# 400 slots in place of 448 for the first wide expert of a token-routed block, and the test that allows it

## The chip, the core and the metric

The kernel runs on one core of a Trainium2 chip. The metric is the device time of one execution in microseconds (us). Three runs of the kernel before gave 542.45, 544.16 and 544.39 us (median 544.16). The profile is of one more execution, which took 543.53 us by the same clock. Its span, from the first to the last instruction, is 541.8 us; the other 1.7 us lie around it.

## The reference

Three layers follow each other. What matters here is the second, a mixture of experts in which every token goes to exactly one of eight experts:

```python
# attention: 2 sequences x 12 heads x 448 tokens x 64  ->  x of 896 tokens x 768
logits = xn @ en.T / tau
expert_idx = np.argmax(logits, axis=1)
for e in range(E):                       # E = 8
    mask = expert_idx == e
    h = np.maximum(x[mask] @ w1[e], 0.0)       # 768 -> 1024
    out[mask] = gate_w[mask, None] * (h @ w2[e])   # 1024 -> 768
# third layer, all 896 tokens: h = x @ w_in (768 -> 2048), g = s * relu(h)**2 + b, g @ w_out (2048 -> 768)
```

Everything is float32. How many tokens an expert gets depends on the inputs. Evaluated on its default inputs (seed 0), the reference sends 3, 7, 31, 25, 387, 3, 9 and 431 tokens to experts 0 to 7; in the first sequence alone, expert 4 has the most (382 of 448).

## The kernel before

**Attention** fills the first 118 us or so: per pair of heads, scores, tanh, exponentials, sums and the product with v, with the routing logits collected on the way.

**Routing** (lines 490 to 601) counts the tokens of each expert (`cnt`), gives every token a slot number, and sorts the 896 tokens by expert: first the expert with the most tokens in the first sequence (rank 0, called R0), then the small ones, last the largest of the others (rank 1, R1). VectorE (DVE) writes the slot list `idx`, by which GpSimd (POOL) gathers the token rows out of DRAM in seven indirect transfers (line 559). It also writes a small table `tab` with the expert, the first slot, the count and a start for copying back for each rank, and a flag `rare`. Every engine reads `rare` later (line 833) and takes one of two courses: `rest(True)`, the common one, when exactly six experts have 32 tokens or fewer and none has over 448; otherwise `rest(False)`, which finishes any distribution. Both are the same function with another argument, written out twice.

**The experts.** The gathered rows are transposed into `xs` (tokens as columns, 768 features as six tiles of 128). All products are made of three float32r matmuls on a high and a low half (`mm3`, lines 638 to 641), so that a 128x128 weight tile against 448 tokens is three matmuls with 448 columns. R0 always takes slots 0 to 447 and R1 slots 448 to 895, in eight hidden tiles of 128 each: `layer1` (line 701) is 18 matmuls from `xs` into one PSUM bank `hw`, then a relu on ScalarE (ACT, line 717) and the low half on DVE (line 718); `layer2` (line 720) is 18 matmuls from those halves into six PSUM banks `y0` to `y5`. Slots that belong to another expert are overwritten afterwards. Stage `s` of the loop in `rest` (line 840) makes `layer1` of tile `s` and `layer2` of the tile before; stage 0 (`layer1` of R0's tile 0, line 824) is made before the courses part. Stages 1 to 7 are R0, 8 to 15 R1. In stage 8 `layer2` of R0's last tile and its copy out of PSUM (`put_wide`, line 726, by the helper `put`, lines 685 and 687) follow.

**The small experts** have a stretch of 32 slots each. Their two layers (`narrow1`, line 779; `narrow2`, line 795) are put into given stages by the table `STAGE`, as plain float32 matmuls with 32 stationary columns.

**Weights** come in 768 KB transfers from SyncE's (SP) queue into twelve slots in two rings (`rawa`, and the front of `mem`); `pump` issues the next one of a fixed list as soon as a slot's former tile has been used. ACT and DVE split each tile into its halves (`split`, lines 621 to 623).

**The boundary** (lines 870 to 926): the small expert of rank 2 ends, some of R1's neighbours' results are kept aside, and the third layer's input is split into halves (`split_y`), in the common course for the first 448 slots before R1's last `layer2`, so that ACT and DVE work beneath it. The third layer follows to the end.

Of the kernel before, what the change touches and what calls it, by code (L numbers as in the profile page):

```python
# [14 lines left out]
ALU = mybir.AluOpType  # L15
AX = mybir.AxisListType
# [5 lines left out]
B, H, S, D = 2, 12, 448, 64  # L22
NT = B * S
DM = H * D
E = 8
F1 = 1024
F2 = 2048
NF1 = F1 // 128
# [18 lines left out]

NARROW = 32
BACK = 224


GATES = "ppppaaa"
# [7 lines left out]
def tile_kernel(ctx, tc, qk, vp, emb, scal, wp, wi, wo, out, dbg=None):  # L60
    nc = tc.nc
    pe, dve, act, pool, sp = nc.tensor, nc.vector, nc.scalar, nc.gpsimd, nc.sync
# [17 lines left out]
    cnt = const.tile([TQ, E], F32, name="cnt")  # L80
# [7 lines left out]
    rr = const.tile([1, 4], F32, name="rr")  # L88
    isn, back = tv[:, 0], tv[:, 1]
    tab = const.tile([1, 4, E], I32, name="tab")  # L90
    rare = const.tile([1, 1], I32, name="rare")
# [407 lines left out]
    def warm(n):  # L499

        t = ps_x.tile([128, 2, 512], F32, tag="xt", name="warm")
        for _ in range(n):
            pe.matmul(out=t[:, 0, 0:128], lhsT=ident, rhs=ident)
# [42 lines left out]
        pe.matmul(out=iv, lhsT=cm[:, i], rhs=ao[:, 0, i], start=(i == 0), stop=False)  # L546
        pe.matmul(out=iv, lhsT=cm[:, i], rhs=ao[:, 1, i], start=False, stop=(i == NI - 1))
    warm(6)
    dve.tensor_scalar(out=isn, in0=cnt[0:1], scalar1=float(NARROW), scalar2=None, op0=ALU.is_le)
    dve.tensor_copy(out=idx, in_=iv)  # L550

    dve.tensor_reduce(out=rr[:, 0:1], in_=isn, axis=AX.X, op=ALU.add)
    dve.tensor_reduce(out=rr[:, 1:2], in_=cnt[0:1], axis=AX.X, op=ALU.max)
    dve.tensor_scalar(out=rr[:, 2:3], in0=rr[:, 0:1], scalar1=float(E - 2), scalar2=None, op0=ALU.not_equal)
    dve.tensor_scalar(out=rr[:, 3:4], in0=rr[:, 1:2], scalar1=float(S), scalar2=None, op0=ALU.is_gt)
    dve.tensor_tensor(out=rare, in0=rr[:, 2:3], in1=rr[:, 3:4], op=ALU.max)

    xg_t = [mem_y[:, j * DM:(j + 1) * DM] for j in range(NS)]
    rows_in += [pool.indirect_dma_start(out=xg, out_offset=None, in_=xd[:, :],
# [34 lines left out]
    for p in range(2):  # L594
        dve.tensor_scalar(out=idx2[:, p], in0=iv, scalar1=2.0, scalar2=float(p), op0=ALU.mult, op1=ALU.add)
    dve.tensor_scalar(out=back, in0=off[0:1], scalar1=-float(BACK), scalar2=0.0, op0=ALU.add, op1=ALU.max)
    for k, row in ((1, off[0:1]), (2, cnt[0:1]), (3, back)):
        dve.tensor_tensor(out=rv[:, k], in0=rm, in1=bc(row, E, 1), op=ALU.mult)
    with nc.allow_low_precision(reason="whole numbers below 1000"):
        dve.tensor_reduce(out=tab, in_=rv, axis=AX.X, op=ALU.add)  # L600
    xctx.close()


# [17 lines left out]
    def split(src, w, lo=dve):  # L621
        act.copy(out=w[0], in_=src)
        lo.tensor_tensor(out=w[1], in0=src, in1=w[0], op=ALU.subtract)

    def split1(u, f, lo=dve):
        key = (u, 0, f // 2)
        src = raw_t[key].rearrange("p (q k c j) -> p c k q j", q=4, k=KD, c=2)[:, f % 2]
        split(src, [t.rearrange("p k (q j) -> p k q j", q=4) for t in W1[f % 2]], lo)
        if f % 2:
            done(key)  # L630

    def split2(u, f, lo=dve):
        key = (u, 1, f // 2)
        split(raw_t[key].rearrange("p (c k f) -> p c k f", c=2, k=KD)[:, f % 2], W2[f % 2], lo)
        if f % 2:
            done(key)

    def mm3(out, ah, al, bh, bl, start, stop, **kw):
        pe.matmul(out=out, lhsT=ah, rhs=bh, start=start, stop=False, **kw)  # L639
        pe.matmul(out=out, lhsT=ah, rhs=bl, start=False, stop=False, **kw)  # L640
        pe.matmul(out=out, lhsT=al, rhs=bh, start=False, stop=stop, **kw)  # L641
# [41 lines left out]
    def put(i, out, in_):  # L683
        if i == 0:
            act.copy(out=out, in_=in_)
        else:
            dve.tensor_copy(out=out, in_=in_)


    def accs():  # L690
        return [ps_y.tile([128, 512], F32, tag=f"y{k}", name=f"y{k}") for k in range(KD)]

    def at(o, n):
        return slice(o, o + n) if isinstance(o, int) else bass.ds(o, n)

    def within(o, low):
        if isinstance(o, int):
            return o
        return nc.s_assert_within(o, 0, NT - low - 1, skip_runtime_bounds_check_because="the expert has more tokens here")

    def layer1(f, n, low, o, hw=hw):


        o = within(o, low)
        wh, wl = W1[f % 2]
        if f == 0 and hw is hn:

            for k in range(KD):
                for w in (wh, wl):
                    pe.matmul(out=hw[:, 0:n], lhsT=w[:, k], rhs=xs[0][:, k, at(o, n)], start=(k == 0 and w is wh), stop=False)  # L710
            for k in range(KD):
                pe.matmul(out=hw[:, 0:n], lhsT=wh[:, k], rhs=xs[1][:, k, at(o, n)], start=False, stop=(k == KD - 1))
        else:
            for k in range(KD):
                mm3(hw[:, 0:n], wh[:, k], wl[:, k], xs[0][:, k, at(o, n)], xs[1][:, k, at(o, n)], k == 0, k == KD - 1)
        hh, hl = (t[:, 0:n] for t in H2[f % 2])
        act.activation(out=hh, in_=hw[:, 0:n], func=ACTF.Relu)
        dve.scalar_tensor_tensor(out=hl, in0=hw[:, 0:n], scalar=0.0, in1=hh, op0=ALU.max, op1=ALU.subtract)

    def layer2(f, n, acc):  # L720
        wh, wl = W2[f % 2]
        hh, hl = (t[:, 0:n] for t in H2[f % 2])
        for k in range(KD):
            mm3(acc[k][:, 0:n], wh[:, k], wl[:, k], hh, hl, f == 0, f == NF1 - 1)

    def put_wide(n, low, o, acc, cnt=None):

        o = within(o, low)
        for k in range(KD):
            yk = y[k % 2][:, k // 2]  # L730
            if cnt is not None:
                keep = scr[:, k % 2 * 224:(k % 2 + 1) * 224]
                rest = yk[:, bass.ds(nc.s_assert_within(o + cnt, 0, NT, skip_runtime_bounds_check_because="slots of an expert"), 224)]
                put(k % 2, keep, rest)
            put(k % 2, yk[:, at(o, n)], acc[k][:, 0:n])
            if cnt is not None:
                put(k % 2, rest, keep)

    def put_last(acc, kept, o_back):
# [3 lines left out]
        for i in range(2):  # L743
            put(i, y[i][:, :, bass.ds(o_back, BACK)], kept[i])

# [23 lines left out]
    def tokens32(r):  # L769
        o = tabv(1, r, NT, [ENG.DVE])  # L770
        dve.tensor_tensor(out=x32, in0=xs[0][:, :, bass.ds(o, 32)], in1=xs[1][:, :, bass.ds(o, 32)], op=ALU.add)
# [31 lines left out]
    def convert(nm, f, out):  # L803

        t = raw_t[nm, f]
        lo, hi = t[:, :, 0], t[:, :, 1]
        o = out.bitcast(I32)
        dve.tensor_scalar(out=o, in0=hi, scalar1=3, scalar2=0x3FFFFFF8, op0=ALU.logical_shift_left, op1=ALU.bitwise_and)
        dve.scalar_tensor_tensor(out=o, in0=hi, scalar=-0x40000000, in1=o, op0=ALU.bitwise_and, op1=ALU.bitwise_or)  # L809
        dve.scalar_tensor_tensor(out=o, in0=lo, scalar=29, in1=o, op0=ALU.logical_shift_right, op1=ALU.bitwise_or)  # L810
        done((nm, f))
# [4 lines left out]
    def cube(t):  # L816
        return t.rearrange("p (k f) -> p k f", k=KD)
# [18 lines left out]

    def rest(fast):

        acc = accs()
        for s in range(1, 2 * NF1):  # L840
            f = s % NF1
            kind, r = STAGE.get(s - 1, (0, 0))
            if kind == 1:
                tokens32(r)
            if s == 2 * NF1 - 2:
                convert("wi", 0, wc0)
                split(cube(wc0), nw)
            elif s == 2 * NF1 - 1:
                convert("wi", 1, wc)
            u, o_ = ("R1", NT - S) if s >= NF1 else ("R0", 0)  # L850
            if s + 1 < 2 * NF1:
                split1("R1" if s + 1 >= NF1 else "R0", (s + 1) % NF1)
            split2(u, f)
            pump()
            if kind:
                (narrow1 if kind == 1 else narrow2)(r)
                pump()

            layer1(f, S, 0, o_)
            if f:  # L860
                layer2(f - 1, S, acc)
            if s == NF1:
                layer2(NF1 - 1, S, acc)
                put_wide(S, 0, 0, acc)
                acc = accs()
            if s >= NF1 and tys:
                r = max(tys)
                put_narrow(tys[r], tabv(1, r, NT, [ENG.Activation, ENG.DVE]))
                last_ty.append(tys.pop(r))
# [19 lines left out]

        o_back = tabv(3, 1, NT - BACK, [ENG.Activation, ENG.DVE])  # L890
        kept = raw_tile(("kept", 0), "b")[:, 0:6 * BACK].rearrange("p (i k t) -> p i k t", i=2, k=3)
        kept = [kept[:, i] for i in range(2)]
        for i in range(2):
            put(i, kept[i], y[i][:, :, bass.ds(o_back, BACK)])

# [7 lines left out]
        else:  # L903
# [3 lines left out]
            for r in range(E):  # L907
                n = tabv(2, r, NT, allc)
# [108 lines left out]
        for n in range(2 * NF):  # L1017
            p, f = divmod(n, NF)
# [25 lines left out]
    with tc.If(rare_v < 1):  # L1044
        rest(True)
# [59 lines left out]
```

## Time and profile before

| | |
|---|---|
| runs | 542.45, 544.16, 544.39 us |
| profiled execution | 543.53 us, span 541.8 us |
| mean granted TensorE clock | 0.987 of full speed |
| TensorE (PE) matmuls | 515.1 us busy, 95% of the span |
| PE weight loads | 418.1 us, 77% |
| DVE, ACT, POOL | 61%, 43%, 8% |
| DMA | 93.42 MB, 172 GB/s on average |

Busy shares are averages over stages with different limits. A row of the trace in order of time gives the start and the length of an instruction, or of several merged ones with their count; a bracket at its end gives how long the engine had been idle before it and what ended that. The ends of matmuls are modelled and neighbours overlap, so the pace of a row of matmuls is read from their starts. L with a number is a line of the kernel before.

### The profile page before, as it was taken

The page shows a single profiled execution, that of the slowest core. Times are in us where ns is not written, and L with a number is a line of the kernel's source. Part 1 is how long each engine was busy: PE and PEld are TensorE (multiplying, and loading weights), DVE is VectorE, ACT ScalarE, POOL GpSimd, SP SyncE. Part 2 cuts the span into 40 slices and gives each one's busy share as a digit, 9 for nine tenths or more (in the row PEclk, how much of TensorE's full clock was granted, in tenths as well). Part 3 has the DMA queues.
Part 4 walks back from the last instruction along what each step waited for, and adds up shares of the span by engine and source line. Part 5 has one row for each costly group of instructions (what it writes and reads, how often), then busy time and mean ns, then how long its engine had stood idle before and what let it go on. Part 6 is the DMA issues. An engine that isn't in the chain of part 4 may idle for free.

```text
span 541.8 us, 7919 instructions
## 1 busy us (share of the span) xinstructions
PE 515.1 (95%) x3136; PEld 418.1 (77%) x3136; DVE 330.0 (61%) x461; ACT 231.7 (43%) x318; POOL 43.5 (8%) x49
## 2 busy tenths in 40 slices
PE   6999998968899999999999899999999999999994
PEld 2344343447788888878888799999999999999994
DVE  2887788875642232432454976666668677887741
ACT  7888987852822221422134422222125333354330
POOL 2000000006430000000001100000000000150013
PEclk9999999988899999999999999999999999999998
DMA  5232542935979699879975133333223233320002
GB/s 174 106 112 58 179 126 54 421 99 189 321 230 376 209 404 365 341 250 406 389 274 197 58 124 110 118 116 117 94 93 113 110 117 116 117 105 1 2 15 92
DMA packets 30365, 93.42 MB, mean 172 GB/s; under 512 B 2376, under 2 KB 16008, under 8 KB 30320
## 3 DMA queue, kind: packets, MB, share of 16 engines
q1 hardware_dynamic: 28816, 87.30, 45.9%
q0 software_dynamic: 1488, 5.51, 2.9%
q8 instruction: 26, 0.43, 0.3%
q14 instruction: 19, 0.16, 0.1%
q10 hardware_dynamic: 16, 0.02, 0.0%
HBM read 87.32 MB, written 5.51 MB: 171 GB/s over the span
## 4 chain that ended last, share of the span: by engine, by line
PE 76%; issue 10%; ACT 5%; DVE 4%; POOL 2%; DMA 2%; POOLq 0%; ACTq 0%; DVEq 0%
PE hw L639 8%; PE hw L640 7%; PE hw L641 7%; PE y L641 6%; PE y L639 6%; PE y L640 6%; PE o L280 4%; PE s L239 4%; PE hn L639 3%; PE hn L640 3%; PE hn L641 3%; PE hn L795 3%; PE hn L779 3%; POOL out_dram L1011 2%; PE s L241 2%
## 5 line engine op out<-in xcount | busy, mean ns | idle before, releaser
L244 ACT ACTIVATE ew<-s,fscale 128x896 f32<-128x896 f32 (+1 forms) x48 | 41.7, 910 | 14.6 <-PE s L239 13.0
L949 ACT ACTIVATE xs<-mem,sc 128x896 fp32r<-128x896 f32 x31 | 32.4, 1044 | 21.5 <-PE y L640 10.5
L969 DVE SCALAR_TENSOR_TENSOR mem<-scr,sc 128x448 f32<-128x448 f32 x32 | 21.6, 681 | 32.2 <-ACT scr L968 32.2
L239 PE MATMUL s<-mem 64*128 64x448 f32 x144 | 36.3, 610 | 5.1 <-DMA mem<-in_qk_dram 4.3
L248 ACT ACTIVATE ew<-ew,sc 128x1792 f32<-128x1792 f32 (+1 forms) x24 | 38.4, 1601 | 0.8
L950 DVE SCALAR_TENSOR_TENSOR xs<-mem,sc,xs 128x896 fp32r<-128x896 f32 x31 | 34.4, 1146 | 3.1 <-ACT xs L949 1.6
L270 DVE RECIPROCAL ew<-su 128x448 f32<-128x448 f32 x12 | 35.4, 2951 | 1.1 <-PE su L266 1.1
L639 PE MATMUL hw<-xs,w11h 128*128 128x448 f32 x90 | 33.8, 375 | 0.0
L239 PEld LDWEIGHTS s<-mem 64*128 64x128 f32 x144 | 12.8, 200 | 26.9 <-issue 11.2
L640 PE MATMUL hw<-xs,w11h 128*128 128x448 f32 x90 | 33.0, 366 | 0.0
L641 PE MATMUL hw<-xs,w11l 128*128 128x448 f32 x90 | 32.9, 365 | 0.0
L280 PE MATMUL o<-ew,mem 128*64 128x448 f32 x144 | 29.7, 547 | 3.3 <-ACT sq L314 1.9
L640 PE MATMUL y<-w21l,xs 128*128 128x384 f32 x96 | 32.5, 338 | 0.0
L639 PE MATMUL y<-w21h,xs 128*128 128x384 f32 x96 | 32.5, 338 | 0.0
L641 PE MATMUL y<-w21h,xs 128*128 128x384 f32 x96 | 32.5, 338 | 0.0
L639 PE MATMUL hw<-xs,w10h 128*128 128x448 f32 x84 | 31.4, 374 | 0.0
L810 DVE SCALAR_TENSOR_TENSOR wc<-rawa,wc 128x768 int32<-128x768 int32 x32 | 30.7, 959 | 1.1
L809 DVE SCALAR_TENSOR_TENSOR wc<-rawa,wc 128x768 int32<-128x768 int32 x32 | 30.7, 959 | 1.1
L640 PE MATMUL hw<-xs,w10h 128*128 128x448 f32 x84 | 30.8, 366 | 0.0
L641 PE MATMUL hw<-xs,w10l 128*128 128x448 f32 x84 | 30.7, 365 | 0.0
L641 PE MATMUL y<-w20h,xs 128*128 128x384 f32 x90 | 30.5, 338 | 0.0
L639 PE MATMUL y<-w20h,xs 128*128 128x384 f32 x90 | 30.5, 338 | 0.0
(299 smaller groups left out, 1205.2 us busy)
## 6 DMA issues: line engine op xcount, KB each, us to landing
rawa<-in_wp_dram SPq DMA_DIRECT2D x32, 768.0 KB, 8.2
mem<-in_wp_dram SPq DMA_DIRECT2D x32, 768.0 KB, 8.6
rawa<-in_wi_dram SPq DMA_DIRECT2D x16, 768.0 KB, 4.9
rawa<-in_wo_dram SPq DMA_DIRECT2D x16, 768.0 KB, 4.3
mem<-in_qk_dram SPq DMA_DIRECT2D x12, 480.0 KB, 3.5
mem<-in_vp_dram SPq DMA_DIRECT2D x12, 256.0 KB, 3.8
xd<-x SPq DMA_DIRECT2D x2, 896.0 KB, 5.0
xd<-x SPq DMA_DIRECT2D x1, 448.0 KB
```

Source lines behind the costliest of these rows:

```text
L239: pe.matmul(out=s[:, i, 0:S], lhsT=kq[ps, kc], rhs=kq[ps, KC:], start=True, stop=True)
L244: act.activation(out=weights(g)[:, 2 * u:2 * u + n], in_=s[:, 0:n, 0:S], func=ACTF.Tanh, scale=fscale[:, 0:1])
L248: act.activation(out=e, in_=e, func=ACTF.Exp, scale=sc[:, 0:1])
L270: dve.reciprocal(out=rs_room(g), in_=su_t.pop(g))
L280: pe.matmul(out=o[64 * i:64 * i + 64], lhsT=v[:, i * 192 + u * 64:i * 192 + u * 64 + 64], rhs=e[:, 2 * u + i], start=(u == 0), stop=False, ...
L639: pe.matmul(out=out, lhsT=ah, rhs=bh, start=start, stop=False, **kw)
L640: pe.matmul(out=out, lhsT=ah, rhs=bl, start=False, stop=False, **kw)
L641: pe.matmul(out=out, lhsT=al, rhs=bh, start=False, stop=stop, **kw)
L809: dve.scalar_tensor_tensor(out=o, in0=hi, scalar=-0x40000000, in1=o, op0=ALU.bitwise_and, op1=ALU.bitwise_or)
L810: dve.scalar_tensor_tensor(out=o, in0=lo, scalar=29, in1=o, op0=ALU.logical_shift_right, op1=ALU.bitwise_or)
L949: act.activation(out=hh, in_=h[:, f, ns], func=ACTF.Identity, bias=sc[:, 3:4])
L950: dve.scalar_tensor_tensor(out=hl, in0=h[:, f, ns], scalar=sc[:, 3:4], in1=hh, op0=ALU.add, op1=ALU.subtract)
```

## The change

The common course gives R0 slots 0 to 399 only. In stages 1 to 8 its `layer1`, `layer2` and the copy out of PSUM run over 400 columns; stage 0 keeps 448, and so does R1. A third condition is added for that course: the count of rank 0, read from `tab`, must not exceed 400. Since `tab` is made later than the place where `rare` was computed, the whole computation of `rare` moves behind `tab`; one comparison and one maximum are added to it.

```diff
--- before.py
+++ after.py
@@ -47,6 +47,8 @@
 
 NARROW = 32
 BACK = 224
+
+SW = 400
 
 
 GATES = "ppppaaa"
@@ -546,14 +548,7 @@
         pe.matmul(out=iv, lhsT=cm[:, i], rhs=ao[:, 0, i], start=(i == 0), stop=False)
         pe.matmul(out=iv, lhsT=cm[:, i], rhs=ao[:, 1, i], start=False, stop=(i == NI - 1))
     warm(6)
-    dve.tensor_scalar(out=isn, in0=cnt[0:1], scalar1=float(NARROW), scalar2=None, op0=ALU.is_le)
     dve.tensor_copy(out=idx, in_=iv)
-
-    dve.tensor_reduce(out=rr[:, 0:1], in_=isn, axis=AX.X, op=ALU.add)
-    dve.tensor_reduce(out=rr[:, 1:2], in_=cnt[0:1], axis=AX.X, op=ALU.max)
-    dve.tensor_scalar(out=rr[:, 2:3], in0=rr[:, 0:1], scalar1=float(E - 2), scalar2=None, op0=ALU.not_equal)
-    dve.tensor_scalar(out=rr[:, 3:4], in0=rr[:, 1:2], scalar1=float(S), scalar2=None, op0=ALU.is_gt)
-    dve.tensor_tensor(out=rare, in0=rr[:, 2:3], in1=rr[:, 3:4], op=ALU.max)
 
     xg_t = [mem_y[:, j * DM:(j + 1) * DM] for j in range(NS)]
     rows_in += [pool.indirect_dma_start(out=xg, out_offset=None, in_=xd[:, :],
@@ -598,6 +593,15 @@
         dve.tensor_tensor(out=rv[:, k], in0=rm, in1=bc(row, E, 1), op=ALU.mult)
     with nc.allow_low_precision(reason="whole numbers below 1000"):
         dve.tensor_reduce(out=tab, in_=rv, axis=AX.X, op=ALU.add)
+    dve.tensor_scalar(out=isn, in0=cnt[0:1], scalar1=float(NARROW), scalar2=None, op0=ALU.is_le)
+
+    dve.tensor_reduce(out=rr[:, 0:1], in_=isn, axis=AX.X, op=ALU.add)
+    dve.tensor_reduce(out=rr[:, 1:2], in_=cnt[0:1], axis=AX.X, op=ALU.max)
+    dve.tensor_scalar(out=rr[:, 2:3], in0=rr[:, 0:1], scalar1=float(E - 2), scalar2=None, op0=ALU.not_equal)
+    dve.tensor_scalar(out=rr[:, 3:4], in0=rr[:, 1:2], scalar1=float(S), scalar2=None, op0=ALU.is_gt)
+    dve.tensor_scalar(out=rr[:, 0:1], in0=tab[:, 2, 0:1], scalar1=float(SW), scalar2=None, op0=ALU.is_gt)
+    dve.tensor_tensor(out=rr[:, 2:3], in0=rr[:, 2:3], in1=rr[:, 3:4], op=ALU.max)
+    dve.tensor_tensor(out=rare, in0=rr[:, 2:3], in1=rr[:, 0:1], op=ALU.max)
     xctx.close()
 
 
@@ -836,7 +840,9 @@
 
     def rest(fast):
 
+
         acc = accs()
+        n0 = SW if fast else S
         for s in range(1, 2 * NF1):
             f = s % NF1
             kind, r = STAGE.get(s - 1, (0, 0))
@@ -847,7 +853,7 @@
                 split(cube(wc0), nw)
             elif s == 2 * NF1 - 1:
                 convert("wi", 1, wc)
-            u, o_ = ("R1", NT - S) if s >= NF1 else ("R0", 0)
+            u, n, o_ = ("R1", S, NT - S) if s >= NF1 else ("R0", n0, 0)
             if s + 1 < 2 * NF1:
                 split1("R1" if s + 1 >= NF1 else "R0", (s + 1) % NF1)
             split2(u, f)
@@ -856,12 +862,12 @@
                 (narrow1 if kind == 1 else narrow2)(r)
                 pump()
 
-            layer1(f, S, 0, o_)
+            layer1(f, n, 0, o_)
             if f:
-                layer2(f - 1, S, acc)
+                layer2(f - 1, n, acc)
             if s == NF1:
-                layer2(NF1 - 1, S, acc)
-                put_wide(S, 0, 0, acc)
+                layer2(NF1 - 1, n0, acc)
+                put_wide(n0, 0, 0, acc)
                 acc = accs()
             if s >= NF1 and tys:
                 r = max(tys)
```

On DVE, at the slot list, the flag's instructions stood around and behind `idx`. Names: `tv` holds which experts are small, `rr` the partial conditions, `gt` and `key` belong to the gates and the ranks that are made next. Before:

```order
L542 TENSOR_TENSOR lg<-lg,nrm 112x64 [waits DVE_49]
L549 TENSOR_SCALAR tv<-cnt 1x8
L550 CAST idx<-iv 128x7 [waits PE_49]
L552 TENSOR_REDUCE rr<-tv 1x1 [waits DVE_49]
L553 TENSOR_REDUCE rr<-cnt 1x1
L554 TENSOR_SCALAR rr<-rr 1x1 [waits DVE_49]
L555 TENSOR_SCALAR rr<-rr 1x1 [waits DVE_49]
L556 TENSOR_TENSOR rare<-rr 1x1 [waits DVE_49]
L569 TENSOR_REDUCE gt<-ex 112x8 [waits Activation_49]
L570 SCALAR_TENSOR_TENSOR key<-cnt,f_128 112x8
```

Now, on the same engine, they stand between the table and the first low half of the transposed tokens (`xs`):

```order
L593 TENSOR_TENSOR rv<-rm,tv 1x64 [waits DVE_49]
L595 TENSOR_REDUCE tab<-rv 1x32 [waits DVE_49]
L596 TENSOR_SCALAR tv<-cnt 1x8
L598 TENSOR_REDUCE rr<-tv 1x1 [waits DVE_49]
L599 TENSOR_REDUCE rr<-cnt 1x1
L600 TENSOR_SCALAR rr<-rr 1x1 [waits DVE_49]
L601 TENSOR_SCALAR rr<-rr 1x1 [waits DVE_49]
L602 TENSOR_SCALAR rr<-tab 1x1 [waits DVE_49]
L603 TENSOR_TENSOR rr<-rr 1x1 [waits DVE_49]
L604 TENSOR_TENSOR rare<-rr 1x1 [waits DVE_49]
L673 TENSOR_TENSOR xs_740<-xt,xs_739 128x6x128 [waits Activation_49] x3
```

Six instructions left the place at `idx` (one of them ahead of it) and eight stand behind `tab`; L602 is the new comparison, L603 the new maximum.

On PE, at the end of stage 1 and the start of stage 2, the matmuls keep their number and order. Before:

```order
L639 MATMUL y_1050<-hh0h,w20h 128x448
L640 MATMUL y_1050<-hh0l,w20h 128x448
L641 MATMUL y_1050<-hh0h,w20l 128x448
L639 MATMUL hw<-xs_739,w10h 128x448
L640 MATMUL hw<-xs_740,w10h 128x448
```

Now:

```order
L643 MATMUL y_1052<-hh0h,w20h 128x400
L644 MATMUL y_1052<-hh0l,w20h 128x400
L645 MATMUL y_1052<-hh0h,w20l 128x400
L643 MATMUL hw<-xs_739,w10h 128x400
L644 MATMUL hw<-xs_740,w10h 128x400
```

Only the number of columns differs. No instruction moves on PE, ACT, POOL or SP.

## Rows read from the trace of the kernel before

**Rows 1.** The page: busy time of each engine, its share, its instructions.

```profile
PE 515.1 (95%) x3136; PEld 418.1 (77%) x3136; DVE 330.0 (61%) x461; ACT 231.7 (43%) x318; POOL 43.5 (8%) x49
```

**Rows 2.** Stretches, R0 to R1's start: window; busy PE, PEld, DVE, ACT, POOL; clock; DMA share; GB/s.

```profile
146.00:187.00 41.00, 41.00 (x322) 34.39 (x321) 16.20 (x22) 11.94 (x18) 7.75 (x4) 1.00 0.77 266
187.00:230.00 43.00, 43.00 (x348) 36.45 (x350) 15.56 (x24) 12.29 (x21) 0.00 (x0) 1.00 0.99 373
```

**Rows 3.** PE in time order: R0's layer2 in stage 1, layer1 in stage 2.

```profile
149.88 0.36 PE L639 MATMUL y<-hh0h,w20h 128*128 128x448 f32 x1
...
153.32 0.37 PE L641 MATMUL y<-hh0h,w20l 128*128 128x448 f32 x1
...
156.65 0.37 PE L640 MATMUL hw<-xs,w10h 128*128 128x448 f32 x1
...
159.92 0.36 PE L641 MATMUL hw<-xs,w10l 128*128 128x448 f32 x1
```

**Rows 4.** PE in time order: 18 matmuls with 384 columns, third layer.

```profile
470.03 0.34 PE L639 MATMUL y<-w21h,xs 128*128 128x384 f32 x1
...
473.03 0.34 PE L641 MATMUL y<-w21h,xs 128*128 128x384 f32 x1
```

**Rows 5.** Line 640's weight loads, experts, then third layer: ns min/median/max.

```profile
L640 PEld LDWEIGHTS y<-hh0l,w20h x48: 187/188/188, 149.9 to 287.7; 128*128 128x128 f32 x48
```
```profile
L640 PEld LDWEIGHTS y<-w21l,xs x96: 187/188/188, 421.8 to 533.4; 128*128 128x128 f32 x96
```

**Rows 6.** PE and DVE in time order, stage 7: layer2's start, low half.

```profile
208.49 0.36 PE L639 MATMUL y<-hh0h,w20h 128*128 128x448 f32 x1
```
```profile
209.32 0.62 DVE L718 SCALAR_TENSOR_TENSOR hh1l<-hw,hh1h 128x448 fp32r<-128x448 f32 x1 [3.50 <-ACT hh1h L717]
```

**Rows 7.** DVE in time order: slot list, flag, table, first low half.

```profile
125.13 0.17 DVE L550 CAST idx<-iv 128x7 int32<-128x7 f32 x1 [0.20 <-PE iv L547]
125.21 0.14 DVE L552 TENSOR_REDUCE rr<-tv 1x1 f32<-1x8 f32 x1
...
125.63 0.15 DVE L556 TENSOR_TENSOR rare<-rr 1x1 int32<-1x1 f32 x1
...
130.04 0.41 DVE L600 TENSOR_REDUCE tab<-rv 1x32 int32<-1x256 f32 x1
136.35 3.15 DVE L669 TENSOR_TENSOR xs<-xt,xs 128x768 fp32r<-128x768 f32 x4 [5.90 <-ACT xs L668]
```

**Rows 8.** PE in time order: transposes of the second and third gather.

```profile
131.50 2.92 PE L664 MATMUL xt<-dgs,mem 128*128 128x128 f32 x24 [0.42 <-DMA mem<-xd,idx]
```

**Rows 9.** SP's queue; its transfers of 192 to 196; PE using them.

```profile
192.62 1.63 SPq L143 DMA_DIRECT2D rawa<-in_wp_dram  x3
```
```profile
rawa<-in_wp_dram SPq DMA_DIRECT2D x3, 768.0 KB, 11.7
```
```profile
212.90 2.13 PE L795 MATMUL hn<-rawa,scr 128*32 128x192 f32 x48
```

**Rows 10.** PE in time order, stage 0; then that stretch's window.

```profile
140.22 0.57 PE L710 MATMUL hn<-xs,w10l 128*128 128x448 f32 x1
140.60 0.57 PE L710 MATMUL hn<-xs,w10h 128*128 128x448 f32 x1
```
```profile
139.00:142.00 3.00, 3.00 (x10) 2.70 (x10) 1.06 (x3) 2.66 (x4) 0.00 (x0) 0.50 1.01 338
```

**Rows 11.** The boundary: ACT, DVE and PE in time order; last, the chain.

```profile
292.82 2.90 ACT L880 CAST xs<-mem 128x448 fp32r<-128x448 f32 x6
```
```profile
298.38 1.67 DVE L687 COPY mem<-y 128x448 f32<-128x448 f32 x3
300.09 0.85 DVE L687 COPY mem<-mem 128x672 f32 x1
```
```profile
294.91 0.36 PE L639 MATMUL hw<-xs,nwh 128*128 128x448 f32 x1
```
```profile
292.42 0.40 issue
```

## The prediction

> **What bounds the kernel now.** I read the page first, then the stretches, then single instructions. The page puts matmuls on TensorE at 95% of the span [rows 1]. A busy share alone proves little, since the ends of matmuls are modelled. So I looked at the stretch that the change touches, the first wide expert R0 and the start of the second, 146 to 230 us: there PE has no idle time at all, while DVE and ACT are busy for well under half and POOL hardly [rows 2]. The third thing to see there is DMA: 77% of its capacity in the first half of the stretch, 99% in the second. PE sets the pace, but the weights arrive on a queue that has nothing to spare.
>
> How long one matmul keeps PE is read from starts. In layer2, 18 matmuls of 448 columns start from 149.88 to 153.32: 3.44 us over 17 intervals, 202.4 ns each. In layer1, 17 of them start from 156.65 to 159.92: 3.27 over 16, 204.4 ns [rows 3]. The mean is 203.4 ns. The third layer has the same type of matmul with 384 columns: 3.00 us over 17 intervals, 176.5 ns [rows 4]. Hence 26.9 ns for 64 columns, 0.42 ns for each, which is one column per cycle at 2.4 GHz (the granted clock in R0's stretch is 1.00 [rows 2]); what is left over, some 17 ns a matmul, is the same at both sizes.
>
> **The change, part by part.**
>
> *Fewer columns.* Seven stages of layer1 (1 to 7) and eight tiles of layer2 (stages 1 to 8) shrink, 18 matmuls each: 15 x 18 = 270 matmuls. Each loses 48 columns, 48 x 0.42 = 20.2 ns, and comes to 183 ns. The sum is 270 x 20.2 = 5.45 us. All of it lies on the path, because PE is never idle there and everything after it follows PE. The bounds, if 400 columns behave like either neighbour: 448's price gives 0, 384's price gives 270 x 26.9 = 7.3 us. I take the line between them: two sizes that agree on the constant to a fraction of a nanosecond leave little room for a step.
>
> *What must still fit beneath PE.* There is one PSUM bank `hw`, so a stage's layer1 waits until the relu and the low half of the stage before have read it. In stage 7 DVE is done with it at 209.32 + 0.62 = 209.94, 1.45 us after that stage's layer2 began at 208.49 [rows 6]. The layer2 that covers this shrinks from 18 x 0.202 = 3.64 to 3.3 us. Enough is left. The relu, the low half and the copy out of PSUM get shorter by a ninth; they are off the path and I cost them at nothing. Were their cover gone, they would be worth some 0.06 us per stage.
>
> *Weights.* Each full stage brings the demand forward by 36 x 20.2 ns = 0.73 us, so it is 5.1 us after stage 7 and 5.45 us after stage 8. In the full stretch the tightest rows that I found are the three transfers issued from 192.62 on, which land some 11.7 us later: the last, issued at about 193.9, lands at 205.6. PE uses the ring at 212.90 [rows 9], at the start of stage 8, so 7.3 us later. Seven shortened stages take 5.1 us of that and leave 2.2. Besides, these issues wait for slots that PE's own earlier work frees, five shortened stages on, so they move forward too, if the queue lets them. I cost this at nothing.
>
> *The flag.* Six DVE instructions leave the place at `idx`. Five of them ran behind it, from 125.21 to 125.63, starting about 0.1 us apart: what follows, the gates, gets ready 0.5 us sooner. Nobody waits for it: the second transposes on PE wait for the gathered rows, not for gates [rows 8], and the gather starts on `idx` alone. `idx` itself waited for PE [rows 7], so it comes no sooner for the instruction taken away ahead of it. Eight instructions now follow `tab`. At about 0.1 us each, most of them dependent, they end 0.8 us after `tab`. Ahead of the next DVE work lies an idle time of 5.90 us until 136.35 [rows 7], which hides them eight times over. The flag itself is then ready near 131 us; the engines reach the branch before stage 1, at about 146. SP too reads it after the table and first waits for the gather. Cost nothing; bounds +0.8 (cover gone) and -0.5 us (if the gates were waited for).
>
> *Around the boundary.* Everything there hangs on PE's stages and moves as a whole.
>
> **Sum.** The profiled execution took 543.53 us; less 5.45 it is 538.1. The three runs have their median 0.6 higher, at 544.16, which would give 538.7. I forecast **538.5 us**, 1.0% faster. About 0.5%, or 2.7 us, is what a measurement of this kernel can tell from no change.
>
> **The rivals.**
>
> *Weight loads set the pace.* Each matmul has its own weight load, recorded with 188 ns [rows 5]. If loads could not follow each other faster than that, a 400-column matmul would take 188 ns rather than 183, and the gain would be 270 x (203.4 - 188) = 4.2 us: 539.6. The same load of the same size has 188 ns beside the 384 columns [rows 5], where the pace is 176.5 ns [rows 4]. So a record longer than the pace does not hold PE up. The Trainium skill, page "Perfetto Trace Analysis", section "Identifying the Most-Contended Engine", says to judge TensorE's headroom by the busy share of weight loads and not of matmuls; by that rule the R0 stretch, with its loads at 84% of the time, has some room left but not the whole of this change's. The trace of the third layer speaks against it here. Chance 0.06.
>
> *The clock falls once more.* Just ahead of stage 1 the granted clock is 0.50 for some 3 us and the matmuls of stage 0 start 0.38 us apart instead of 0.20 [rows 10], after PE had stood idle for the transposes. With the gates ready sooner, PE's work before that place moves by up to 0.5 us and its idle times change. One such stretch more costs some 9 matmuls x 0.17 = 1.5 us: 540.0; one fewer gives 537.0. Nothing says that it must move. Chance 0.06.
>
> *The weights come late.* DMA is at 99% [rows 2], and the demand moves forward by more than the queue can follow. Each transfer that lands late stops PE in the stage that uses it. At worst the whole gain is returned: 543.5, no change. Against it stands the margin of 2.2 us above and that no wait on a transfer ends an idle time of PE there. Chance 0.04.
>
> *The other course is taken.* This is the slower case. The new condition holds as long as rank 0 has at most 400 tokens. By the reference's default inputs it has 387, 13 below. At 401 the flag is set and every engine runs `rest(False)`: R0 stays at 448 columns, so the gain is gone; and the split of the third layer's input no longer lies beneath R1's last layer2 but behind it. PE goes straight on to the third layer at 294.91 now. Then it would wait for the copies out of PSUM, 1.67 + 0.85 = 2.5 us, and for the first of the six splits with its low half, about 1 us (2.90 / 6 on ACT, as much again on DVE). Between them stand eight reads of the table with a branch each; the nearest row is the 0.40 us of issue in the chain around such a read [rows 11], so 3.2 us. That makes 543.5 + 2.5 + 1 + 3.2 = 550.2 us. Chance 0.04: the count could differ if the inputs timed were others than the default.
>
> **How the numbers follow.** The forecast has 0.80, the rivals 0.06, 0.06, 0.04 and 0.04. The range takes in the forecast from either base (538.1 from the profile, 537.0 from the lowest run of 542.45, 538.9 from the highest), the weight loads (539.6) and the clock either way (537.0 to 540.0); with half a microsecond of scatter at either end it is 536.7 to 540.5, and leaves out the late weights and the other course. Faster by over 0.5%: 0.80 + 0.06 + 0.06, less a little for weights partly late, 0.91. Within 0.5%: 0.05. Slower: 0.04.
>
> **What the profile of the changed kernel would show.** Right: 128x400 matmuls that start 183 ns apart in both layers, no idle time on PE from stage 1 to the boundary, and the narrow block that is now at 212.90 some 5.1 us sooner relative to stage 1; the rest of the gain in stage 8's layer2; the stretch from the boundary on unchanged in length. DVE shows the flag's eight instructions between `tab` and the first `xs`, inside idle time. Wrong: a pace of 188 ns (weight loads), idle time on PE in front of a narrow or wide block that a transfer ends (weights), a low clock at another place, or matmuls of R0 with 448 columns in stage 1 (the other course).

## The result, and the profile after

The changed kernel takes 538.12 us (median of 537.21, 537.69, 538.56 and 538.9) against 543.78 for the kernel before, timed beside it. The ratio is 0.9892, with an interval of 0.9856 to 0.9927: 1.1% faster. The forecast was 538.5. The profiled execution took 538.56 us.

The page of the changed kernel, beside [rows 1]: PE's matmuls are 5.2 us shorter, the other engines are within 0.6 us of what they were.

```profile
span 536.8 us, 7918 instructions
...
PE 509.9 (95%) x3136; PEld 417.7 (78%) x3136; DVE 330.2 (62%) x463; ACT 231.1 (43%) x318; POOL 43.5 (8%) x49
```

Stretches of the changed kernel, columns as in [rows 2]: R0's stages to 187 us, then on to R1's first ones, and last 7 us around stage 0. In the first two PE has no idle time at either side of the change. The same 41 us now hold 342 matmul records where they held 322. In the third the granted clock is 0.51, so half for nearly the whole stretch.

```profile
146.00:187.00 41.00, 41.00 (x342) 36.91 (x341) 17.37 (x25) 13.54 (x21) 8.16 (x5) 1.00 0.82 291
187.00:225.00 38.00, 38.00 (x340) 33.10 (x342) 14.15 (x23) 11.11 (x19) 0.00 (x0) 1.00 1.02 391
136.00:143.00 7.00, 6.20 (x22) 5.81 (x23) 3.59 (x5) 4.87 (x8) 0.00 (x0) 0.51 0.96 326
```

The same 7 us in the kernel before, with 0.76:

```profile
136.00:143.00 7.00, 5.64 (x24) 5.12 (x25) 3.71 (x5) 5.86 (x10) 0.01 (x1) 0.76 0.95 318
```

PE of the changed kernel in time order, for [rows 3] and [rows 9]: layer2 of stage 1 (first and last of 18), layer1 of stage 2 (the second and the last of 18), stage 8's narrow block, and the first matmul of stage 9, which is R1's with 448 columns.

```profile
150.06 0.34 PE L643 MATMUL y<-hh0h,w20h 128*128 128x400 f32 x1
...
153.12 0.34 PE L645 MATMUL y<-hh0h,w20l 128*128 128x400 f32 x1
...
156.41 0.34 PE L644 MATMUL hw<-xs,w10h 128*128 128x400 f32 x1
...
159.34 0.35 PE L645 MATMUL hw<-xs,w10l 128*128 128x400 f32 x1
...
208.01 2.13 PE L799 MATMUL hn<-rawa,scr 128*32 128x192 f32 x48
...
217.11 0.36 PE L643 MATMUL hw<-xs,w11h 128*128 128x448 f32 x1
```

Layer2's starts are 3.06 us apart over 17 intervals, 180.0 ns each; layer1's 2.93 us over 16, 183.1 ns. Before it was 202.4 and 204.4 [rows 3]. PE's first matmul of stage 1 starts at 146.67, so stages 1 to 8 take 217.11 - 146.67 = 70.44 us. Before they took from 146.12 to 222.41, 76.29 us. **The change in these stages is -5.85 us**, 270 matmuls by 21.7 ns.

The span shrank by 5.0 us, not 5.85. Two other places differ. Everything up to the routing's transposes came 0.59 us sooner (a matmul of the attention's end stands at 116.92 for 117.51), and from there to stage 1 it took 1.14 us longer. In that second piece lies the half clock of stage 0, which lasts longer in this execution than in the one before (0.51 for 0.76 above). What follows stage 9 took 0.30 us more.

### The profile page after: what moved, and what is told of

Same layout as the page of the kernel before. It is cut to its first block, busy times and chain, and to the rows that moved or that the text cites. A ratio compares the mean times of both kernels' runs of the same rounds, so it can differ in the third digit from the quotient of the medians.

```text
span 536.8 us, 7918 instructions
## 1 busy us (share of the span) xinstructions
PE 509.9 (95%) x3136; PEld 417.7 (78%) x3136; DVE 330.2 (62%) x463; ACT 231.1 (43%) x318; POOL 43.5 (8%) x49
## 4 chain that ended last, share of the span: by engine, by line
PE 73%; issue 10%; ACT 7%; DVE 4%; POOL 2%; another core or an unknown queue 2%; DMA 1%; POOLq 0%; ACTq 0%; DVEq 0%
PE hw L643 8%; PE hw L645 7%; PE hw L644 7%; PE y L645 6%; PE y L644 6%; PE y L643 6%; PE o L282 5%; PE s L241 4%; PE hn L645 3%; PE hn L643 3%; PE hn L644 3%; PE hn L799 3%; PE hn L783 3%; POOL out_dram L1017 2%
## 5 line engine op out<-in xcount | busy, mean ns | idle before, releaser
L643 PE MATMUL hw<-xs,w11h 128*128 128x448 f32 (+1 forms) x90 | 33.2, 369 | 0.0
L645 PE MATMUL hw<-xs,w11l 128*128 128x448 f32 (+1 forms) x90 | 32.6, 363 | 0.0
L644 PE MATMUL hw<-xs,w11h 128*128 128x448 f32 (+1 forms) x90 | 32.3, 359 | 0.0
L643 PE MATMUL hw<-xs,w10h 128*128 128x448 f32 (+1 forms) x84 | 31.0, 369 | 0.0
L645 PE MATMUL hw<-xs,w10l 128*128 128x448 f32 (+1 forms) x84 | 30.5, 363 | 0.0
L644 PE MATMUL y<-w20l,xs 128*128 128x384 f32 x90 | 30.5, 338 | 0.0
```

## The experiments

Each kernel was timed beside the kernel before on the same chip. Its median was 543.76 us in the first group (the flag alone, the columns alone, the other course, the idle matmuls), 541.94 in the second (384, 256, 392 with 432, and the latter with idle matmuls) and, on another chip, 539.37 in the third (the last three below). Groups are therefore compared by ratio. A number "stages 1 to 8" is read like the 70.44 above.

### Only the flag moved

```diff
-        n0 = SW if fast else S
+        n0 = S
```

> Half of the change: the flag moves behind the table with its third condition, R0 keeps 448 columns in all stages. Theory (the columns are all of it): as the kernel before, 543.2 to 544.2 us, ratio within 0.1%; stages 1 to 8 as long as before (76.3 us from stage 1's first matmul to stage 9's); the flag is ready near 130.5 us in idle time of DVE. Rival A (the earlier gates help): 0.5 us less. Rival B (the move of the flag changes PE's idle times and so lengthens the stretch at half clock, as the changed kernel's profile has it, 6.8 us against 3.4): 1 to 1.5 us more, 545.

543.79 us in 12 runs, ratio 0.9995 (0.9973 to 1.0017). Stages 1 to 8 take 76.28 us. The flag's new place and its two extra instructions give and cost nothing that this interval, about 1.2 us either way, can show; a half microsecond either way would be hidden in it.

### Only the columns

The kernel before, flag at its old place and without the third condition:

```diff
+        n0 = 400 if fast else S
...
-            u, o_ = ("R1", NT - S) if s >= NF1 else ("R0", 0)
+            u, n, o_ = ("R1", S, NT - S) if s >= NF1 else ("R0", n0, 0)
...
```

`layer1`, `layer2` and `put_wide` take `n` and `n0` as in the changed kernel.

> The other half: R0 takes 400 columns in stages 1 to 8 of the common course, the flag is computed where it was and without the third condition. Theory: stage 1 to stage 9 take 70.4 us as in the changed kernel, the time is that of the changed kernel, 537.5 to 538.7. Rival B (the flag's move costs 1 us there): 537.0 or less. Rival A (the move helps): 538.7 or more.

537.09 us, ratio 0.9866 (0.9826 to 0.9905), stages 1 to 8 70.43 us: the whole gain, with columns alone. The half clock ahead of stage 1 tells more. The same 7 us around stage 0, first with only the flag moved, then with only the columns (one fence each):

```profile
136.00:143.00 7.00, 5.74 (x25) 5.29 (x26) 3.71 (x5) 5.29 (x9) 0.00 (x0) 0.76 0.98 316
```
```profile
136.00:143.00 7.00, 6.27 (x23) 5.89 (x24) 3.52 (x5) 4.87 (x8) 0.00 (x0) 0.53 1.02 347
```

The long half-clock stretch (0.53 against the changed kernel's 0.51) stands where the flag was not moved, and the short one (0.76) where it was. So the flag does not lengthen it. The kernel before, with the flag unmoved, had 0.76 as well. The columns, which become fewer only after this stretch, do not set it either: with 256 of them (below) it is 0.76 again.

### The other course

```diff
-SW = 400
+SW = 384
```

R0's 387 tokens then exceed the limit, and `rest(False)` runs.

> The changed kernel with the limit at 384 in place of 400, so that R0's 387 tokens exceed it and every engine takes the other course. Theory of the prediction: R0 at 448 columns, the boundary longer by 2.5 us of copies, 1 us of the first split and 8 x 0.4 us of table reads and branches: 550.2 us. Rival (reads and branches are nearly free): 547. Rival (branches cost much more than the 0.4 us of issue, on four engines): 555 or more. Then PE stands idle in front of the third layer for the difference.

593.78 us, ratio 1.0911 (1.0844 to 1.0977): 50 us slower, where I had priced 6.7; the rival with dear branches holds. The third layer's first matmul starts at 346.81 for 294.91 before. Two pieces make up the 51.9 us. PE of this kernel at the boundary, then ACT:

```profile
346.81 0.71 PE L643 MATMUL hw<-xs,nwh 128*128 128x448 f32 x1 [41.23 <-ACT w11h L626]
```
```profile
343.10 2.90 ACT L886 CAST xs<-mem 128x448 fp32r<-128x448 f32 x6 [36.77 <-PEq L920]
```

PE is idle for 41.23 us, and ACT's split, which PE needs, waits for PE's own sequencer at line 920 (`PEq`). The branches of the two groups of reads, by engine: count, then ns min/median/max.

```profile
L916 PEldq COMPARE_BRANCH  x2: 3517/4020/4522, 302.1 to 306.4; - x2
L916 ACTq COMPARE_BRANCH  x2: 45/48/50, 305.9 to 306.8; - x2
L916 DVEq COMPARE_BRANCH  x2: 56/62/69, 306.7 to 307.8; - x2
```
```profile
L920 ACTq COMPARE_BRANCH  x6: 45/45/45, 307.8 to 320.5; - x6
L920 DVEq COMPARE_BRANCH  x6: 56/56/56, 308.9 to 323.8; - x6
L920 PEldq COMPARE_BRANCH  x6: 4002/4069/6872, 311.7 to 338.8; - x6
```

On PE each of the eight branches is recorded with 3.5 to 6.9 us. They follow each other, about 35 us in sum (8.0 for the two, some 27 for the six). On ACT and DVE the record is 45 to 69 ns, but that is not what a branch costs there. The first instructions behind the six branches, two each:

```profile
L920 ACTq EVENT_SEMAPHORE  x12: 17/17/17, 311.1 to 322.6; - x12
L920 DVEq EVENT_SEMAPHORE  x12: 21/21/21, 313.4 to 324.1; - x12
```

ACT's first branch of the six begins at 307.8 and its next instruction at 311.1; on DVE it is 308.9 and 313.4. Taken over all eight branches, the next instruction comes 0.1 to 5.5 us after the record's end, 12.8 us in sum on either engine. So these engines pay as well, behind the record and less than PE, and they are done at 324, long before PE at 343.

The other piece, 10.6 us, arises at the entry: the narrow block of stage 2 starts at 164.12 for 153.48 with the flag alone. Line 1050 chooses the course. PE's branch there, in this kernel and then in the changed one (there twice, the second at the end of the course):

```profile
L1050 PEldq COMPARE_BRANCH  x1: 4943/4943/4943, 145.0 to 145.0; - x1
```
```profile
L1050 PEldq COMPARE_BRANCH  x2: 86/138/189, 145.4 to 525.5; - x2
```

At the choice the common course falls through in 0.09 us; the other one jumps, in 4.9 us. Stage 1's first matmul then starts at 150.26, 4.3 us later than with the flag alone. The rest of the 10.6 us arises in stage 1, where the granted clock is 0.51 from 151 to 160 us and PE waits for DVE's and POOL's sequencers at line 1050, 0.7 and 0.8 us.

The Trainium skill, page "Runtime: NRT & Kernel Launch", section "Instruction fetch mechanics", says that a taken branch to code outside the current window stalls until that code is fetched by DMA. The trace agrees. Five of PE's branches begin between 319 and 343 us, and these are the instruction transfers of that window on one queue (number, MB, share):

```profile
q8 instruction: 10, 0.16, 3.6%
```

That is two for each branch. Why PE's branches cost more than ACT's and DVE's, no run here shows.

### 384 columns, then 256, with the same operands

```diff
-        n0 = SW if fast else S
+        n0 = 384 if fast else S
```

The limit stays at 400, so the common course is taken. This kernel leaves out 3 of R0's 387 tokens, the one with 256 columns 131; they serve to read the pace.

> The changed kernel with 384 columns for R0 in stages 1 to 8, the limit still 400, so that 3 of R0's 387 tokens are left out. It puts 384 columns on the very operands of R0. Measured so far at the starts: layer2 202.4 ns at 448 columns and 180.0 at 400, so 0.467 ns a column. Theory (one column per cycle, and the constant left over does not grow again): layer2 172.5 to 173.3 ns, layer1 176 to 177; stages 1 to 8 shorter by another 270 x 7 ns = 1.8 us; 536.2. Rival (176.5 ns, the pace of the third layer at 384 columns, is a floor set by the weight loads): layer2 at 176.5, gain 0.9 us or less, 537.2.

534.65 us, ratio 0.9867 (0.9841 to 0.9893), stages 1 to 8 68.51 us. A layer2 of R0, first and last of 18:

```profile
165.75 0.34 PE L643 MATMUL y<-hh0h,w20h 128*128 128x384 f32 x1
...
168.69 0.33 PE L645 MATMUL y<-hh0h,w20l 128*128 128x384 f32 x1
```

2.94 us over 17 intervals, 172.9 ns: 3.6 ns less than the third layer's 176.5 with the same number of columns [rows 4]. The operands differ: here the weights (`w20h`) stand still in the array and the activations (`hh0h`) move through it, in the third layer's rows the activations (listed as `xs`) stand still and the weights (`w21h`) move. So my second point of the line lay on another line.

```diff
-        n0 = SW if fast else S
+        n0 = 256 if fast else S
```

> The same with 256 columns, so 131 of R0's tokens are left out. Theory (one column per cycle): matmuls start about 121 ns apart where nothing else is waited for, and stages 1 to 8 need 270 x 60 = 16.2 us less than with 400 columns, 522 us, less what the weights give back: DMA is then asked for 16 us more than the 2.2 us of margin that the prediction counted, so PE should stand idle for transfers in stages 6 to 8, some 5 to 10 us, and the time is 526 to 533. Rival 1 (weight loads, recorded with 188 ns, set a floor near 176 ns): 537 and no waits on transfers. Rival 2 (the weights keep up): 522, no idle time on PE.

526.31 us in one run, with 541.94 before. PE in time order: a layer2, first and last of 18, then stage 7's narrow block.

```profile
167.19 0.28 PE L643 MATMUL y<-hh1h,w21h 128*128 128x256 f32 x1
...
169.22 0.28 PE L645 MATMUL y<-hh1h,w21l 128*128 128x256 f32 x1
...
184.81 0.62 PE L783 MATMUL hn<-mem,scr 128*32 128x256 f32 x2 [0.34 <-DMA mem<-in_wp_dram]
187.77 0.64 PE L783 MATMUL hn<-mem,scr 128*32 128x256 f32 x1 [2.34 <-DMA mem<-in_wp_dram]
```

Two things follow. The pace is 2.03 us over 17 intervals, 119.4 ns, while its weight loads are recorded with 191 ns, here those of line 644 in that `layer2` and another, 150 to 184 us (count, then busy us and mean ns):

```profile
L644 PEld LDWEIGHTS y<-hh1l,w21h 128*128 128x128 f32 x18 | 3.4, 191 | 0.0
```

The record is no floor. And here at last the weights bind. Seen from the changed kernel's 180 and 183 ns, 119 and 118 ns on 270 matmuls should give 17.0 us; stages 1 to 8 took 59.88 us, 10.6 less. Of the missing 6.4 us, 5.5 are in stage 7's narrow block, which took 8.26 us instead of 2.72. Only about half of them are PE's waits for transfers, 0.34 and 2.34 us above. After the second wait the granted clock is half for 3.2 us, and the block's matmuls start 0.42 us apart for 0.21:

```profile
187.70:190.90 3.20, 3.13 (x32) 1.54 (x36) 0.00 (x0) 0.00 (x0) 0.00 (x0) 0.50 1.00 409
```

So here a late transfer cost more than its wait. Another 0.7 us is a wait for DVE ahead of stage 2's narrow block. The stretches of this kernel show the DMA share (second column from the right):

```profile
146.00:187.00 41.00, 38.39 (x443) 32.37 (x441) 20.16 (x30) 14.64 (x24) 8.31 (x5) 1.00 0.95 349
187.00:215.00 28.00, 27.23 (x258) 21.90 (x262) 9.88 (x17) 7.89 (x15) 0.00 (x0) 0.94 1.03 402
```

### Both wide experts at their own size

392 columns for R0, and 432 for R1, which has 431 tokens:

```diff
-SW = 400
+SW = 392
+SW1 = 432
...
-            u, n, o_ = ("R1", S, NT - S) if s >= NF1 else ("R0", n0, 0)
+            u, n, o_ = ("R1", n1, NT - n1) if s >= NF1 else ("R0", n0, 0)
...
```

The condition on the largest count, R1's last `layer2` and its copy out of PSUM take the new size too.

> The same idea carried on within the counts of these inputs: R0 with 392 columns (limit 392, it has 387), and R1 with 432 columns in stages 8 to 15 at slots 464 to 895 (limit 432, it has 431). Theory: R0's 270 matmuls lose 8 columns, R1's 288 lose 16, at 0.42 to 0.467 ns: 0.9 to 1.0 and 1.9 to 2.2 us; together 3 us less than the changed kernel, 535.0. Rival (the weights, at 99% of DMA, now come late): PE idle in front of a narrow block and 536 or more.

534.86 us, ratio 0.9860 (0.9840 to 0.9880). That is 0.3% under the changed kernel's ratio, 1.7 us for the 3 that I expected; the two intervals overlap. The stages themselves gave nearly the whole of it: from stage 1's first matmul to the third layer's it is 140.10 us in this kernel's profile and 142.95 in the changed one's, 2.85 us less. R1's layer2 in stage 9, first and last of 18, 3.33 us over 17 intervals, 195.9 ns:

```profile
219.54 0.36 PE L644 MATMUL y<-hh0h,w20h 128*128 128x432 f32 x1
...
222.87 0.36 PE L646 MATMUL y<-hh0h,w20l 128*128 128x432 f32 x1
```

The paces of layer2 on the experts' operands are now known at six sizes:

| columns | 448 | 432 | 400 | 392 | 384 | 256 |
|---|---|---|---|---|---|---|
| ns per matmul | 202.4 | 195.9 | 180.0 | 177.6 | 172.9 | 119.4 |
| ns beyond columns / 2.4 GHz | 15.7 | 15.9 | 13.3 | 14.3 | 12.9 | 12.7 |

### Idle matmuls ahead of stage 0

Ten matmuls on `ident` in front of the last group of transposes, to fill PE's idle time before stage 0:

```diff
+        if j == 3:
+            idle = ps_h.tile([128, 512], F32, tag="h0", name="idle")
+            for _ in range(10):
+                pe.matmul(out=idle[:, 0:128], lhsT=ident, rhs=ident)
```

> The changed kernel with ten idle 128x128 matmuls of the identity on PE ahead of the transposes of the fourth gather, into a PSUM bank that is free there; they fill about 1.2 us of PE's idle time in front of stage 0. Theory: this idle time is what takes the clock to half, so the stretch at 0.50 ahead of stage 1 gets shorter or goes; stage 0's 18 matmuls then take 3.7 to 4.4 us rather than 5.4 and the time falls by 1 to 2 us, to 536 to 537. Rival (the clock falls all the same, or the matmuls delay the transposes by as much): 538 to 539.

536.48 us, ratio 0.9862 (0.9824 to 0.9899), in its profile without a half clock there (1.00 from 136 to 143 us). But the kernel with columns alone, in the same group, had 537.09, its runs (535.7 to 538.72) around these (535.99 to 537.5). The same ten matmuls on top of 392 and 432 columns:

> The 392 and 432 columns together with the ten idle matmuls ahead of the fourth gather's transposes. Theory: the two gains add up, since one lies before stage 1 and one behind it: 3 us and 1.6 us from 538.1, so 533.5. Rival (with the clock up earlier the weights of the first stages come late, or the clock falls all the same): 535 or more.

533.33 us, ratio 0.9838 (0.9818 to 0.9857), and 1.5 us less than the kernel without them (534.69 to 535.53 there, 532.91 to 534.49 here). It is the lowest ratio of all kernels that leave no token out. Yet the half clock was also absent from the profile of 384 columns, which has no idle matmuls. So the changed kernel, the columns alone and the idle matmuls went together to a chip once more:

> The changed kernel once more, beside its two neighbours on one chip. Theory (the flag's new place costs nothing, and the microsecond between this kernel and the one with fewer columns alone is scatter of the clock ahead of stage 1): ratio to the kernel before within 0.2% of that of the kernel with fewer columns alone. Rival (the flag behind the table costs about a microsecond once the columns are fewer): 1 us or 0.2% slower than that kernel, in most of the runs.

> Fewer columns with the flag at its old place, on the same chip as the changed kernel. Theory: the same time as the changed kernel within 0.2%, 538 us with the kernel before at 543.8. Rival: 1 us less than the changed kernel.

> The changed kernel with ten idle matmuls ahead of stage 0, which change no output, on the same chip as the changed kernel. Theory (they keep the clock up through stage 0): 1 to 2 us less than the changed kernel, and a narrower scatter, as one cause of scatter is gone. Rival (the clock ahead of stage 1 varies whatever PE does there): the same time as the changed kernel within 0.1%, same scatter.

The changed kernel: 533.49 us, ratio 0.9890 (0.9872 to 0.9907). The columns alone: 534.17, ratio 0.9904 (0.9885 to 0.9922). With the idle matmuls: 535.45, ratio 0.9932 (0.9916 to 0.9948). The ratio of the changed kernel repeats. It is 0.7 us faster than the columns alone, not 1 us slower, so the rival falls; most of the 0.7 us stands in the two profiles already at the end of attention (116.97 against 117.59 for the matmul named above), ahead of the flag's place. But the idle matmuls now cost 2.0 us, where they had seemed to give. ACT and PE of the changed kernel in time order, ACT first as in the result's profile, then ACT and PE on the third group's chip:

```profile
134.96 2.20 ACT L672 CAST xs<-xt 128x768 fp32r<-128x768 f32 x3 [9.68 <-remote]
```
```profile
130.63 0.80 ACT L672 CAST xs<-xt 128x768 fp32r<-128x768 f32 x1 [5.30 <-PE xt L668]
```
```profile
131.65 4.39 PE L668 MATMUL xt<-dgs,mem 128*128 128x128 f32 x36 [1.05 <-DMA mem<-xd,idx]
```

On that chip ACT copies the first transposes as soon as PE has made them, PE runs the other 36 in one go, the clock stays at 1.00, and stage 1 starts at 141.51 instead of 146.67. In all three profiles of this group ACT's first copy starts at 130.6 to 131.5 us; in all ten others at 134.9 to 135.9, eight of them from one other chip, two (the result's and the one before) from a chip that is not on record. So what leaves PE idle ahead of stage 0 is a late start of ACT, and these profiles part by chip, not by kernel: three kernels stand on both sides. The semaphore events of the traces, which no view above shows, put the delay ahead of ACT. ACT's copy waits for a semaphore that PE raises when a group of transposes is done. In this group it rises within 0.02 us of the first group's end (130.60 for 130.59 in the changed kernel). In the ten others three such signals come together, just before ACT starts: at 134.93, 135.06 and 135.19 in the result's profile, where the first transposes had ended at 130.52. Where the delay is absent there is no idle time to fill, and ten matmuls more are 2.40 us of PE's time:

```profile
134.22 2.40 PE L683 MATMUL idle<-ident 128*128 128x128 f32 x20
```

With them stage 1 starts at 143.54, 2.03 us later: the whole loss.

## Why the prediction was right

**Right.** PE sets the pace, and the gain is columns. The kernel with columns alone has all of it, the one with the flag alone none. Every stage after the boundary moved as a whole: the third layer's first matmul went from 294.91 [rows 11] to 289.62, 5.29 us sooner, and what follows kept its length within 0.3 us. The narrow block of [rows 9] starts 5.44 us sooner relative to stage 1, for 5.1 forecast.

**A term mis-sized.** I forecast 183 ns and 5.45 us; the stages gave 180.0 in layer2, 183.1 to 184.4 in layer1, and 5.85 us. The step that failed is "two sizes that agree on the constant to a fraction of a nanosecond leave little room for a step". The two sizes agreed by chance: the third layer's matmuls have other operands and 16.5 ns beyond their columns, the experts' have 12.9 at the same 384. On their own operands the remainder falls from 15.7 ns at 448 columns to 12.7 at 256, not evenly. What makes it up was not tried. That the time came out 0.4 us from the forecast is in part luck: in the profiled execution the stages gave 0.4 us more than forecast, and the places outside them, which the sum held unchanged, took back 0.85. Two bounds are also off by their own sums: 537.0 less half a microsecond is 536.5, not 536.7, and 4.2 us of gain in place of 5.45 puts the weight loads at 539.75, not 539.6. Neither matters for the result.

**Weights.** Right, with more room than I gave. SP's queue of the changed kernel issues the three transfers of [rows 9] at 189.29 instead of 192.62, since the slots come free sooner, and they take as long as before:

```profile
189.29 1.63 SPq L145 DMA_DIRECT2D rawa<-in_wp_dram  x3
```
```profile
rawa<-in_wp_dram SPq DMA_DIRECT2D x3, 768.0 KB, 11.5
```

That is a median; the last of the three, issued at 190.59, takes longest:

```profile
rawa<-in_wp_dram SPq DMA_DIRECT2D x1, 768.0 KB, 12.1
```

It lands at 202.7, and the ring is used from 208.01: 5.3 us of margin, for a forecast of 2.2 without that move. (Before, the last one took 12.3 us and not the median's 11.7, so the forecast's own margin was 1.6.) A DMA share of 1.02 with no wait on PE was therefore no contradiction; at 256 columns the waits came.

**The flag.** DVE of the changed kernel, for [rows 7]:

```profile
124.49 0.17 DVE L551 CAST idx<-iv 128x7 int32<-128x7 f32 x1 [0.23 <-PE iv L549]
124.58 0.22 DVE L564 TENSOR_REDUCE gt<-ex 112x8 f32<-112x64 f32 x1
...
129.27 0.41 DVE L595 TENSOR_REDUCE tab<-rv 1x32 int32<-1x256 f32 x1
129.61 0.17 DVE L596 TENSOR_SCALAR tv<-cnt 1x8 f32<-1x8 f32 x1
...
130.42 0.15 DVE L604 TENSOR_TENSOR rare<-rr 1x1 int32<-1x1 f32 x1
135.79 0.96 DVE L673 TENSOR_TENSOR xs<-xt,xs 128x768 fp32r<-128x768 f32 x1 [5.22 <-ACT xs L672]
```

The gates follow `idx` at once. The eight instructions run from 129.61 to 130.57 and end 0.9 us after `tab` (0.8 forecast), with 5.22 us of idle time behind them. On the third group's chip ACT's copy comes sooner and 1.07 us of that idle time are left: less cover, but enough.

**The rivals.** *Weight loads* fell: 172.9 and 119.4 ns with records of 188 to 191 ns. In the changed kernel's first stretch the loads are busy for 36.91 of 41 us, 90%. The Trainium skill, page "Perfetto Trace Analysis", section "Identifying the Most-Contended Engine", judges TensorE's headroom by the busy share of weight loads, beside the share of peak arithmetic; by that busy share a tenth would be left. 256 columns took a third off the pace, so for these matmuls the measurement decides against it. The prediction also misread its own 84%: the 16% that this leaves are more than the 7.7% that stages 1 to 8 lost, so by that figure the whole change had room. *The clock* did what that rival describes in the profiled execution (0.51 against 0.76 in the same 7 us before), but not for the reason given there: the kernel with the flag at its old place did so too (0.53). *Late weights* did not occur. *The other course* would have been slower as said, but by 50 us and not by 6.7. The step that failed is "eight reads of the table with a branch each; the nearest row is the 0.40 us": that row is of a read in the common course, and a branch that PE takes costs 3.5 to 6.9 us, some ten times as much. The entry into that course I had left out.

**Open.** What holds these signals of PE, and with them ACT's first copy, for some 4 us on one chip and not on the other: the transposes were long done. Also why the clock falls there for a shorter or a longer time on one chip, and why a taken branch costs PE more than ACT and DVE.

## What to carry to other kernels

Where the matmul engine has no idle time, padding is paid by the column, and narrowing a stretch gives its columns back until the weights come late, from where on a wait can bring a stretch at half clock as well; take the price of a column from the same operands, not from another layer. A test that guards the shorter stretch cost nothing that could be measured in the common case, but look at what the fallback costs and how near the limit the data is (387 of 400 here, 9% if it fails). Filling an idle gap to keep a clock up pays only where that gap exists, and here it existed on one chip and not on another.

## What was not expected of the hardware

- A taken branch on PE's queue took 3.5 to 6.9 us, with two instruction transfers for each of the five between 319 and 343 us; one that fell through took 0.09 us. On ACT and DVE the record of a taken one is 45 to 69 ns, but the next instruction came 0.1 to 5.5 us later.
- After a wait of 2.34 us for a transfer PE ran at half clock for 3.2 us (256 columns, stage 7).
- In ten profiles PE's signals for three groups of transposes came together, 4.3 to 4.6 us after the first group's end; in three, all from one other chip, each came at once.
- The kernel before took 543.76, 541.94 and 539.37 us in the three groups, the first two on one chip. In the profiles of the third, the changed kernel reached stage 1 5.2 us sooner than in its first profile (141.51 for 146.67), while its stages 1 to 8 agreed to a hundredth (70.43 for 70.44).
